# RetNet recurrence and softplus-erf MoE block on one core: the first layer of group G0 as 26 products, with its half of W_in summed by ScalarE and accumulating GpSimd transfers

## The chip, the cores and the metric

The kernel runs on one core of a Trainium2 chip, in one launch. The metric is the device time of the execution in microseconds (us); lower is better. The engines are TensorE (PE, with its weight loads PEld), VectorE (DVE), ScalarE (ACT), GpSimd (POOL) and SyncE (SP). Each works through its own queue of instructions in order, and waits on semaphores for what other engines or DMA transfers must have done.

## The reference

A recurrent attention block (RetNet, float32) feeds a block with two matrix products and a gate between them. B, H, S, D are 4, 8, 768, 64; the second block sees 3072 tokens of 512 features, W_in is 512 x 2048 and W_out 2048 x 512. The weights come as 64-bit floats.

```python
for t in range(S):
    state = gamma[None, :, None, None] * state + np.einsum('bhd,bhe->bhde', k[:, :, t], v[:, :, t])
    y[:, :, t] = scale * np.einsum('bhd,bhde->bhe', q[:, :, t], state)
...
x = np.ascontiguousarray(attn_out.transpose(0, 2, 1, 3)).reshape(B * S, H * D)
h = x @ w_in
sp = np.maximum(h, 0.0) + np.log1p(np.exp(-np.abs(h)))
g = h * erf(sp)
return (g @ w_out).astype(np.float32)
```

So softplus and erf are taken of every element of `h`, and everything is computed in float32.

## The kernel before

**Stages.** The recurrence is cut into 24 chunks `j` of 128 positions, each done with products inside the chunk and a state carried from chunk to chunk. The first four chunks give the first 512 tokens, which go through the second block in four groups (g = 0 to 3), one for each 512 of the 2048 hidden features: `hidden(g, u)` makes four tiles of `h`, `gate(g)` takes softplus and erf on ScalarE, `gated(g)` multiplies by `h` on VectorE, and `project(g, tt)` adds to the output of 128 tokens in PSUM. In these early groups the weights are also converted from 64-bit words to float32, in 16 pieces, by VectorE and ScalarE (`conversion`, L313 to L331), from raw buffers that SP's loads fill; four buffers turn, and a load goes out when the piece before it in the same buffer has been read.

The other 2560 tokens go in chunks of 256, two groups for each chunk: group g = G0 + 2i takes half s=0 of the hidden features and the next one half s=1, with G0 = 4 and 24 groups in all. There W_in's half is a 4 x 4 grid of 16 blocks (each 128 x 256 here), and the tokens' x is a 4 x 2 grid. The first layer is done with a fast algorithm: 26 products of sums of blocks (`hidden_steps`, the list `STEPS`), in place of 32 plain ones. For it, `W_SUMS` makes 30 sums of blocks of W_in for each half, in place and in tiles 16 to 25, once in the whole kernel (`sum_in`, L344, on VectorE), and `x_sums` makes 18 sums of blocks of x for each chunk (L933, VectorE). Each product goes to one of four PSUM banks (two named `hp`, two named `r`), and is read from there into `h`: the first time for a block of `h` by ScalarE (L965, L967), afterwards added or subtracted by VectorE (L963). A product that writes a bank waits until the reads of what it held are done. The second layer uses seven products instead of eight (`project_part`, L1034), with four more sums of W_out (T1 to T4) for each half: these are made by a negating ScalarE copy and a GpSimd transfer that adds in its flight (`sums`, L352 and L353). T2 is made from T1, and T4 from T2.

**Group G0 before.** Since the sums of W_in cannot be made before the plain use of W_in in groups 0 to 3 is over, G0's first layer is done plainly (`hidden_plain`, L971 to L985): eight tiles of 4 products with 256 columns. In the meantime VectorE makes half s=1's sums (L1187, L1196, L1200), and half s=0's from L1209 on into group G0+1, by the list `order` (L1241 to L1243). `project(G0 - 1, tt)`, the last part of the first 512 tokens, stands in between, with `put_first`, which copies its output out.

**What sets the order.** The order of instructions is written out by hand (`manual_schedule`): the program's order is each engine's order. In the early groups small steps are paid out at points of `hidden` and `project`: conversion steps by `pace`, other steps by the list `waiting`, in `pace_around`. In the later groups, lists by product number (`order`) say after which product VectorE or ScalarE gets another step: `prepared(j)` scales and transposes a chunk's k and q (five VectorE steps), `g_sums` makes the sums for the second layer, `last_steps` a sum of W_out. `sub_begin(j)`, `sub_states(j)` and `sub_visit(j, g)` do a chunk of the recurrence on TensorE with VectorE's mask and state. `load(j)` puts a chunk's loads on SP's queue.

**Names that come up.** G0 is group 4; half s holds features by `w_in_of` and `w_out_of`. W_in's blocks stand in `w_in_sb[:, s, 0:26]`; tiles 16 to 23 of each half serve as raw buffers for the conversion first, as does part of `w_out_sb` (`spare`, `place`). HS is `h`, E the gate's result. `act`, `ret` and `ps_h` have two buffers of each named tile.

## Time and profile before

| what | before |
| --- | --- |
| median of 3 runs | 662.71 us (662.67 to 663.26) |
| profiled execution, span from the first to the last instruction | 660.9 us |
| granted TensorE clock, mean | 1.000 |
| TensorE busy | 655.7 us |
| VectorE busy | 508.4 us |
| ScalarE busy | 280.2 us |
| GpSimd busy | 11.7 us |
| VectorE's 60 sums of W_in (L344), 128 x 256 each | 0.42 us each |
| G0's plain first layer (L980) | 64 instructions, from 127.6 to 142.7 us |
| first layer of G0+1 (L951) begins | 158.4 us |

The page counts an fp32 matmul as two instructions, so a product of `STEPS`, with its two column halves of the weights, is four, and the 26 products of a group are 104. The profile's times of an engine are the sums of its instructions' durations; matmuls overlap in them, so TensorE's rate is read from the distance between starts. A line in the timeline gives the start, the length of a run of like instructions, the engine, the source line, the operation and the tiles; in square brackets stands how long the engine was idle before it, and what ended the wait. The groups from G0+1 to the last but one follow each other at a distance of 25.9 us (158.4, 184.3, 210.2 us and so on). The DMA engines are busy for 0.83 to 1.17 of the time in every 10 us from 10 to 80 us, and for 0.61 or less in the 30 us after them.

### The profile page before, as it was taken

Reading aid. Unit: us, or ns where it says so; the run is one execution under the profiler, and the core shown is the slowest. Engines: PE = TensorE matmul, PEld = TensorE weight load, DVE = VectorE, ACT = ScalarE, POOL = GpSimd, SP = SyncE. Lnnn points to the kernel's source line nnn. Section 1 sums busy time; section 2 is a strip of 40 time slices with the busy share of each in tenths; the row PEclk is TensorE's granted clock in tenths of the full one; section 3 lists DMA queues with packets and bytes.
Section 4 is the critical chain, followed back from the end, with each engine's and each line's share of the span. In section 5 each row is a group of like instructions: output and inputs, shape, how many; then the busy total and the mean of one; then the engine's idle time right before and its main releaser. Section 6 shows DMA issues by size and latency. Waiting matters only on the chain.

```text
span 660.9 us, 15247 instructions
## 1 busy us (share of the span) xinstructions
PE 655.7 (99%) x6200; PEld 557.3 (84%) x6200; DVE 508.4 (77%) x1102; ACT 280.2 (42%) x402; POOL 11.7 (2%) x29
## 2 busy tenths in 40 slices
PE   8999999999999999999999999999999999999998
PEld 7744444576999999999999999999999999999997
DVE  5999999969986786788678678677687688476464
ACT  3468363445534334244254253342432542533440
POOL 1000000110100000000000000000000000000000
PEclk9999999999999999999999999999999999999999
DMA  9999844385753321222222322221231210000000
GB/s 188 223 264 231 211 129 107 63 152 90 144 123 61 85 47 32 67 47 46 70 44 47 73 39 46 42 72 37 44 79 36 46 53 1 2 34 0 1 33 32
DMA packets 159413, 51.88 MB, mean 78 GB/s; under 512 B 143216, under 2 KB 149744, under 8 KB 159344
## 3 DMA queue, kind: packets, MB, share of 16 engines
q1 hardware_dynamic: 157776, 46.72, 32.8%
q0 software_dynamic: 1152, 4.19, 3.4%
q8 instruction: 48, 0.79, 0.5%
q14 instruction: 21, 0.17, 0.1%
q10 hardware_dynamic: 416, 0.01, 0.0%
HBM read 40.39 MB, written 6.29 MB: 71 GB/s over the span
## 4 chain that ended last, share of the span: by engine, by line
PE 98%; DMA 1%; DVE 0%; ACT 0%; issue 0%
PE o L1034 37%; PE hp L951 22%; PE r L951 12%; PE hp L860 8%; PE o L896 8%; PE hp L980 2%; PE r L736 2%; PE hp L628 1%; PE o L772 1%; PE r L524 1%; PE r L557 1%; PE o L604 1%; PE r L751 1%; PE hp L751 1%; DMA kq<-in_k_dram 1%; PE r L772 0%
## 5 line engine op out<-in xcount | busy, mean ns | idle before, releaser
L1034 PE MATMUL o<-w_out_sb,h 128*128 128x256 f32 (+1 forms) x640 | 142.7, 380 | 0.0
L951 PE MATMUL hp<-xs,w_in_sb 128*128 128x128 f32 x988 | 138.1, 275 | 0.0
L1034 PEld LDWEIGHTS o<-w_out_sb,h 128*128 128x128 f32 x640 | 119.5, 190 | 16.6
L963 DVE TENSOR_TENSOR h<-h,hp 128x256 f32<-128x256 f32 x190 | 78.0, 418 | 70.5 <-PE hp L951 65.6
L951 PEld LDWEIGHTS hp<-xs,w_in_sb 128*128 128x128 f32 x988 | 128.4, 192 | 3.0
L1034 PE MATMUL o<-w_out_sb,e 128*128 128x256 f32 x480 | 113.5, 379 | 0.0
L1034 PEld LDWEIGHTS o<-w_out_sb,e 128*128 128x128 f32 x480 | 86.8, 190 | 9.4
L817 ACT ACTIVATE e<-h 128x2048 f32<-128x2048 f32 x22 | 42.1, 1912 | 119.6 <-DVE h L963 119.6
L963 DVE TENSOR_TENSOR h<-h,r 128x256 f32<-128x256 f32 x152 | 56.9, 415 | 22.3 <-PE r L951 21.4
L965 ACT COPY h<-hp 128x256 f32<-128x256 f32 x38 | 14.2, 373 | 130.7 <-PE hp L951 122.7
L951 PE MATMUL r<-xs,w_in_sb 128*128 128x128 f32 x456 | 63.3, 275 | 0.0
L951 PEld LDWEIGHTS r<-xs,w_in_sb 128*128 128x128 f32 x456 | 57.0, 192 | 0.0
L860 PE MATMUL hp<-xT,w_in_sb 128*128 128x512 f32 (+2 forms) x144 | 56.5, 548 | 0.0
L849 DVE TENSOR_TENSOR e<-h,e 128x1024 f32<-128x1024 f32 x42 | 49.2, 1213 | 8.0 <-ACT e L830 8.0
L860 PEld LDWEIGHTS hp<-xT,w_in_sb 128*128 128x128 f32 x144 | 25.8, 190 | 27.0 <-issue 24.6
L951 PE MATMUL hp<-xT,w_in_sb 128*128 128x128 f32 x304 | 46.3, 275 | 0.0
L951 PEld LDWEIGHTS hp<-xT,w_in_sb 128*128 128x128 f32 x304 | 41.5, 192 | 1.4 <-issue 0.5
L830 ACT ACTIVATE e<-e 128x2048 f32<-128x2048 f32 (+1 forms) x23 | 42.1, 1836 | 0.2
L967 ACT ACTIVATE h<-hp 128x256 f32<-128x256 f32 x57 | 21.9, 384 | 29.7 <-PE hp L951 28.3
L951 PE MATMUL r<-xT,w_in_sb 128*128 128x128 f32 x228 | 31.7, 275 | 0.0
L830 ACT ACT_TABLE_LOAD x24 | 30.8, 1283 | 0.4
L951 PEld LDWEIGHTS r<-xT,w_in_sb 128*128 128x128 f32 x228 | 28.5, 192 | 0.0
(164 smaller groups left out, 799.0 us busy)
## 6 DMA issues: line engine op xcount, KB each, us to landing
w_out_sb<-in_moe_w_out_dram SPq DMA_DIRECT2D x14, 512.0 KB, 5.2
kq<-in_k_dram SPq DMA_DIRECT2D x23, 256.0 KB, 4.0
v<-in_v_dram SPq DMA_DIRECT2D x23, 256.0 KB, 3.4
out_dram<-r SPq DMA_DIRECT2D x23, 256.0 KB, 2.9
kq<-in_q_dram SPq DMA_DIRECT2D x288, 16.0 KB, 1.9
kb<-in_k_dram SPq DMA_DIRECT2D x288, 16.0 KB, 1.8
w_in_sb<-in_moe_w_in_dram SPq DMA_DIRECT2D x8, 512.0 KB, 10.1
w_out_sb<-w_out_sb POOLq DMA_DIRECT2D x8, 512.0 KB, 5.3
```

The source lines that it names most:

```text
L736: nc.tensor.matmul(pp[r][col * D : (col + 1) * D, u % 2, t], x[own, u, :], QT[j][own, u, t], start=first(r, col), stop=True, skip_group_ch ...
L751: nc.tensor.matmul(other[a][own, u % 2, D:] if crossed else pp[a][own, u % 2, t], V[j][t, 2 * u + r, :], AM[j][t, r, u, :D], start=crossed ...
L817: nc.scalar.activation(E[g], HS[g], AF.Softplus)
L830: nc.scalar.activation(E[g][:, half], E[g][:, half], AF.Erf)
L849: nc.vector.tensor_tensor(E[g][:, half], HS[g][:, half], E[g][:, half], op=ALU.mult)
L860: nc.tensor.matmul(HP_[ft][:, t], w_in_of(ft, kk), XC[0][:, kk, t], start=(kk == 0), stop=(kk == n_k - 1),)
L896: nc.tensor.matmul(O[0][tt].rearrange("p (d c) -> p d c", d=2), E[g][:, u * TCH + tt * P : u * TCH + (tt + 1) * P], w_out_of(ft), start=(f ...
L951: nc.tensor.matmul(to[:, u, :], w_in_sb[:, s, w, u * P : (u + 1) * P], XS[m](x), start=first and u == 0, stop=True, skip_group_check=True,)
L963: nc.vector.tensor_tensor(h, h, of, op=ALU.add if plus else ALU.subtract)
L965: nc.scalar.copy(h, of)
L967: nc.scalar.activation(h, of, AF.Copy, scale=-1.0)
L1034: nc.tensor.matmul(O[m][i][:, half, at], G[g][a][:, u * P : (u + 1) * P], w_out_sb[:, s, OUT[b], u, at], start=i not in started, stop=(s = ...
```

## The change

G0's first layer is now `hidden_steps(G0)`, the 26 products, and `hidden_plain` is gone. So half s=0's sums must be there before G0. For that the halves are cut otherwise: s=0 is now the features of groups 0 and 1, s=1 those of groups 2 and 3 (`w_in_of`, `w_out_of`, `conversion`), so W_in's half s=0 has had its plain use after group 1. The new `moved_sums` makes a sum with a ScalarE copy (negating for a difference) into the target tile or into one of two tiles `negated`, and a GpSimd transfer of 128 KB that adds in its flight; where the target is one of the terms of an addition, the transfer alone does it. All 30 sums of half s=0 are made in this way at points of `project` and `hidden` (before and after `pace_around`), and the first 12 of half s=1 during G0's products; VectorE makes the remaining 18 of s=1 (`sum_in(1, n_sums)`). The list of sums is put in another order:

```python
W_SUMS = (
    (17, 8, 10, "-"), (16, 2, 6, "+"), (7, 3, 7, "+"), (4, 4, 17, "+"), (10, 10, 16, "+"),
    (2, 2, 3, "+"), (18, 16, 4, "-"), (8, 12, 8, "-"), (22, 15, 13, "-"), (19, 18, 5, "-"),
    (25, 18, 7, "+"), (3, 3, 15, "-"), (20, 1, 19, "-"), (16, 16, 7, "+"), (4, 4, 6, "-"),
    (20, 0, 20, "+"), (19, 19, 13, "-"), (7, 7, 10, "+"), (21, 9, 20, "+"), (24, 20, 12, "-"),
    (1, 1, 5, "+"), (9, 13, 9, "-"), (12, 17, 12, "-"), (5, 5, 2, "+"), (23, 15, 9, "-"),
    (6, 14, 12, "+"), (15, 2, 15, "-"), (13, 23, 11, "-"), (6, 6, 15, "-"), (13, 13, 7, "-"),
)
```

A row (to, a, b, sign) sets tile `to` to the sum or difference of tiles a and b. Tiles 16 to 23 of half s=0 are written by the sums early, so as a raw buffer they serve once only, and the other three turn (`place`). To make room in SBUF, `am` of the first chunks lies in a tile of the name `r`, and `am` of the later ones has D columns instead of C. In G0 `sub_begin(6)` follows the layer, two calls of `project(G0 - 1, ...)` stand ahead of `sub_visit` instead of one, and `prepared(6)` is paid out after products 6, 8, 10, 13 and 15.

```diff
--- before.py
+++ after.py
@@ -44,35 +44,35 @@
 
 N_W, N_X = 26, 18
 W_SUMS = (
...
@@ -223,11 +223,11 @@
     w_out_sb = const.tile([P, 2, 7, FG, DH], F32, name="w_out_sb")
 
     def w_in_of(ft, kk):
-        half, s, i = ft // (2 * FG), ft % (2 * FG) // FG, ft % FG
+        s, half, i = ft // (2 * FG), ft % (2 * FG) // FG, ft % FG
         return w_in_sb[:, s, 4 * (2 * half + i // 2) + kk, i % 2 * P : (i % 2 + 1) * P]
 
     def w_out_of(ft):
-        half, s, i = ft // (2 * FG), ft % (2 * FG) // FG, ft % FG
+        s, half, i = ft // (2 * FG), ft % (2 * FG) // FG, ft % FG
         return w_out_sb[:, s, 2 * half : 2 * half + 2, i, :]
 
 
@@ -243,7 +243,7 @@
     numbers = halves(spare[0][:, 2 * CE :])
     later = ret.tile([P, N_X, P], F32, name="xs", bufs=1)[:, : CE // P].rearrange("p a f -> p (a f)")
     powers = [halves(spare[1][:, 2 * CE :]), halves(later)]
-    last_power = halves(spare[1][:, :CE])
+    last_power = halves(spare[0][:, :CE])
     pieces = [("in", 0), ("in", 1)]
     for n in range(4):
         if n < 3:
@@ -251,7 +251,7 @@
         pieces += [("out", 2 * n), ("out", 2 * n + 1)]
     n_p = len(pieces)
 
-    place = [n % 4 if n < n_p - 4 else (n - n_p + 4) % 3 for n in range(n_p)]
+    place = (0, 1, 2, 3, 0, 1, 2, 0, 1, 2, 0, 1, 2, 0, 1, 2)
 
     def load_piece(n, *parts):
 
@@ -287,7 +287,7 @@
 
 
         which, i = pieces[n]
-        half, s, at = i // 4, i % 4 // 2, i % 2
+        s, half, at = i // 4, i % 4 // 2, i % 2
 
 
         parts = itertools.product(
@@ -339,14 +339,36 @@
 
     def sum_in(s, upto):
 
-        assert all(("hidden", 2 * FG + s * FG + u) in done for u in range(FG))
+        assert all(("hidden", (2 * s + 1) * FG + u) in done for u in range(FG))
         for to, a, b, sign in W_SUMS[in_sums[s] : upto]:
             nc.vector.tensor_tensor(w_in_sb[:, s, to], w_in_sb[:, s, a], w_in_sb[:, s, b], op=OP[sign])
         in_sums[s] = max(in_sums[s], upto)
 
+    negated = [const.tile([P, 2 * P], F32, name=f"negated{i}") for i in range(2)]
+
+    def moved_sums(s, upto):
+
+
+        assert all(("hidden", (2 * s + 1) * FG + u) in done for u in range(FG))
+        while in_sums[s] < upto:
+            n = in_sums[s]
+            to, a, b, sign = W_SUMS[n]
+            x = w_in_sb[:, s]
+            if sign == "+":
+                if to not in (a, b):
+                    nc.scalar.copy(x[:, to], x[:, b])
+                add = x[:, b if to == a else a]
+            else:
+                minus = negated[n % 2] if to == a else x[:, to]
+                nc.scalar.activation(minus, x[:, b], AF.Copy, scale=-1.0)
+                add = minus if to == a else x[:, a]
+            nc.gpsimd.dma_start(x[:, to], add, accum_op=ALU.add)
+            in_sums[s] += 1
+            yield
+
     def sums(s):
 
-        assert ("project", s) in done
+        assert ("project", 2 * s + 1) in done
         x = {name: w_out_sb[:, s, at] for name, at in OUT.items()}
         for to, a, b in (("T1", "12", "11"), ("T2", "22", "T1"), ("T3", "22", "12"), ("T4", "21", "T2")):
             nc.scalar.activation(x[to], x[b], AF.Copy, scale=-1.0)
@@ -485,6 +507,7 @@
 
     QT, KT, SC, AM, XC, SU = {}, {}, {}, {}, {}, {}
 
+    first_am = act.tile([P, 2, 2, HP, C], F32, name="r", bufs=1)
     psum_turn = itertools.cycle((ps_r, ps_h))
 
 
@@ -879,8 +902,12 @@
         done.add(("hidden", ft))
         if ft == FG - 1:
             need("in", FG + 2)
+        if g > 1:
+            next(moves, None)
         if g:
             pace_around(3.4 if ft > FG else 0)
+        if g > 1:
+            next(moves, None)
 
     def project(g, tt):
         if g == 0 and tt == 0:
@@ -902,7 +929,9 @@
             )
         if step == TT - 1:
             done.add(("project", g))
+        next(moves, None)
         pace_around(3.4)
+        next(moves, None)
 
     def put_first(tt):
         o = E[G0 - 1].rearrange("p (u t c) -> p t u c", u=FG, t=TT)[:, tt]
@@ -968,22 +997,6 @@
                 written.add(o)
             yield
 
-    def hidden_plain(g):
-
-        m, s = chunk_of(g), (g - G0) % 2
-        HS[g] = act.tile([P, N], F32, name="h")
-        h = HS[g].rearrange("p (f t u c) -> p f u t c", f=2, t=2, u=FG)
-        x = XC[m // 2][:, :, m % 2 * SCH : (m % 2 + 1) * SCH]
-        for f, u in itertools.product(range(2), range(FG)):
-            to = ps_h.tile([P, TCH], F32, name="hp")[:, :SCH]
-            for kk in range(n_k):
-                nc.tensor.matmul(
-                    to, w_in_of((2 * f + s) * FG + u, kk), x[:, kk], start=kk == 0, stop=kk == n_k - 1
-                )
-            nc.scalar.copy(h[:, f, u], to.rearrange("p (t c) -> p t c", t=2))
-            yield
-        done.update(("hidden", (2 * f + s) * FG + u) for f in range(2) for u in range(FG))
-
     G = {}
 
     def last_gated(g):
@@ -1148,6 +1161,9 @@
         ],
     ]
 
+    n_sums = len(W_SUMS)
+
+    moves = moved_sums(0, n_sums)
     for g in range(G0):
         for u in range(FG):
 
@@ -1184,42 +1200,41 @@
     nc.gpsimd.memset(idle, 1.0)
 
     j = JPC + 2
-    sum_in(1, 12)
-    all_of(prepared(j))
+    assert in_sums[0] == n_sums
+    moves = moved_sums(1, 12)
+    x_sums(G0)
+    gated(G0 - 1)
     load(j + 2)
-    gated(G0 - 1)
-    for n, _ in enumerate(hidden_plain(G0), start=1):
-        if n in (1, 4, 7):
+    next_chunk = prepared(j)
+    for n, _ in enumerate(hidden_steps(G0), start=1):
+        if n in (6, 8, 10, 13, 15):
+            next(next_chunk, None)
+        if n in (11, 17, 23):
             next(last_steps)
-        if n == 3:
-            sub_begin(j)
-    sum_in(1, 20)
-    x_sums(G0)
+        if n in (4, 8, 13, 15, 19, 21, 25):
+            next(moves, None)
+    all_of(moves)
+    all_of(next_chunk)
+    sub_begin(j)
+    project(G0 - 1, 0)
     sub_states(j)
     all_of(prepared(j + 1))
-    sum_in(1, len(W_SUMS))
-    project(G0 - 1, 0)
     nc.scalar.activation(idle, idle, AF.Softplus)
     gate_softplus(G0)
+    project(G0 - 1, 1)
     sub_visit(j, G0)
     load(j + 3)
     put_first(0)
+    put_first(1)
     gate_erf(G0)
     next(last_steps)
-    sum_in(0, 12)
-    for tt in range(1, TT):
+    sum_in(1, n_sums)
+    for tt in range(2, TT):
         project(G0 - 1, tt)
         put_first(tt)
     gated(G0)
-    sum_in(0, 20)
     j += 1
 
-    def sums_left():
-        for n in range(21, len(W_SUMS) + 1):
-            sum_in(0, n)
-            yield
-
-    w_sums = sums_left()
     put = None
     for g in range(G0 + 1, NG):
         even = (g - G0) % 2 == 0
@@ -1238,9 +1253,6 @@
                 18: (next_chunk, e_sums), 20: (e_sums,), 24: (next_chunk,),
             }
         if g == G0 + 1:
-            order.update({n: (w_sums,) for n in (1, 2, 3, 4)})
-            for n in (14, 16, 18, 20, 24):
-                order[n] += (w_sums,)
             order.update({n: (last_steps,) for n in (11, 17, 23)})
         for n, _ in enumerate(hidden_steps(g), start=1):
             if put is not None and n in (14, 16, 18):
@@ -1257,7 +1269,6 @@
         gate_softplus(g)
         if more:
             sub_visit(j, g)
-        all_of(w_sums)
         if g == G0 + 1:
             all_of(last_steps)
         if g + 1 < NG and not even:
```

Left out of the diff are the rows of `W_SUMS`, given above, and the three places where the later chunks' `am` is read and written with its new shape.

More of the change, by code (lines that the diff above doesn't have):

```diff
@@ L46 @@
 W_SUMS = (
+    (17, 8, 10, "-"),
     (16, 2, 6, "+"),
-    (17, 8, 10, "-"),
+    (7, 3, 7, "+"),
     (4, 4, 17, "+"),
     (10, 10, 16, "+"),
+    (2, 2, 3, "+"),
     (18, 16, 4, "-"),
+    (8, 12, 8, "-"),
+    (22, 15, 13, "-"),
     (19, 18, 5, "-"),
+    (25, 18, 7, "+"),
+    (3, 3, 15, "-"),
     (20, 1, 19, "-"),
+    (16, 16, 7, "+"),
+    (4, 4, 6, "-"),
     (20, 0, 20, "+"),
+    (19, 19, 13, "-"),
+    (7, 7, 10, "+"),
     (21, 9, 20, "+"),
+    (24, 20, 12, "-"),
+    (1, 1, 5, "+"),
     (9, 13, 9, "-"),
-    (22, 15, 13, "-"),
+    (12, 17, 12, "-"),
+    (5, 5, 2, "+"),
     (23, 15, 9, "-"),
-    (7, 3, 7, "+"),
-    (24, 20, 12, "-"),
-    (25, 18, 7, "+"),
-    (2, 2, 3, "+"),
-    (8, 12, 8, "-"),
-    (12, 17, 12, "-"),
-    (3, 3, 15, "-"),
-    (15, 2, 15, "-"),
-    (19, 19, 13, "-"),
-    (16, 16, 7, "+"),
-    (7, 7, 10, "+"),
-    (4, 4, 6, "-"),
-    (1, 1, 5, "+"),
-    (5, 5, 2, "+"),
-    (6, 14, 12, "+"),
+    (6, 14, 12, "+"),
+    (15, 2, 15, "-"),
+    (13, 23, 11, "-"),
     (6, 6, 15, "-"),
-    (13, 23, 11, "-"),
     (13, 13, 7, "-"),
@@ L566, in ret_mask @@
     def ret_mask(j):
-        AM[j] = ret.tile([P, 2, HP, C], F32, name="am")
+        AM[j] = first_am[:, j % 2]
         for s in range(2):
@@ L632, in sub_mask @@
     def sub_mask(j):
-        AM[j] = ret.tile([P, 2, HP, C], F32, name="am")
+        AM[j] = ret.tile([P, 2, HP, D], F32, name="am")
         for s in range(2):
             nc.vector.tensor_tensor(
-                AM[j][:, s, :, :D],
+                AM[j][:, s],
                 SC[j][s][:, :, :D],
@@ L691, in sub_results @@
                         V[j][t, 2 * u + r, :],
-                        AM[j][t, r, u, :D],
+                        AM[j][t, r, u],
                         start=False, stop=True, skip_group_check=True,
@@ L753, in of_values @@
                         V[j][t, 2 * u + r, :],
-                        AM[j][t, r, u, :D],
+                        AM[j][t, r, u],
                         start=crossed or first(r, col), stop=True, skip_group_check=True,
```

## The prediction

> **What bounds the kernel now.** I read the page's engine totals and chain first, then the timelines of TensorE, VectorE, GpSimd and ScalarE round the place of the change.
>
> ```profile
> PE 655.7 (99%) x6200; PEld 557.3 (84%) x6200; DVE 508.4 (77%) x1102; ACT 280.2 (42%) x402; POOL 11.7 (2%) x29
> PE 98%; DMA 1%; DVE 0%; ACT 0%; issue 0%
> ```
>
> TensorE is the bound everywhere, at a granted clock of 1.00 in every window. So a change pays by the TensorE time that it removes, less every gap that it opens. TensorE's timeline (start, duration, line, count) at G0, the group whose first layer changes:
>
> ```profile
> 127.60 5.34 PE L980 MATMUL hp<-xT,w_in_sb 128*128 128x256 f32 x24
> ...
> 133.96 8.90 PE L980 MATMUL hp<-xT,w_in_sb 128*128 128x256 f32 x40
> 142.70 3.60 PE L896 MATMUL o<-w_out_sb,r 128*128 128x512 f32 x8
> ...
> 148.00 10.57 PE L896 MATMUL o<-w_out_sb,r 128*128 128x512 f32 x24
> 158.41 0.61 PE L951 MATMUL hp<-xT,w_in_sb 128*128 128x128 f32 x4
> ```
>
> The plain layer (L980) is 64 instructions; with chunk 6's scores between (132.87 to 133.96, 1.09 us) it takes 142.70 - 127.60 - 1.09 = 14.01 us. In the L951 rows a product (4 instructions) starts each 0.445 us. VectorE before the next group (G0+1):
>
> ```profile
> 148.75 0.41 DVE L797 TENSOR_TENSOR state<-state,r 128x256 f32<-128x256 f32 x1
> 149.08 4.85 DVE L344 TENSOR_TENSOR w_in_sb<-w_in_sb 128x256 f32<-128x256 f32 x12
> 153.85 2.35 DVE L849 TENSOR_TENSOR e<-h,e 128x1024 f32<-128x1024 f32 x2
> 156.12 4.47 DVE L344 TENSOR_TENSOR w_in_sb<-w_in_sb 128x256 f32<-128x256 f32 x12
> 160.91 0.42 DVE L963 TENSOR_TENSOR h<-h,hp 128x256 f32<-128x256 f32 x1 [0.31 <-PE hp L951]
> 163.11 0.68 DVE L537 TENSOR_TENSOR kq<-kq,kq_s 128x512 f32<-128x512 f32 x1
> 163.71 1.41 DVE L963 TENSOR_TENSOR h<-h,r 128x256 f32<-128x256 f32 x4
> ```
>
> VectorE is free of its sums at 160.6, and G0+1's product 5 is there for it at 160.8: by 0.3 us it isn't late. A sum costs 4.77/12 to 4.47/12, mean 0.39 us; a PSUM read (L963) occupies 0.42 and gives way after 0.33. GpSimd's accumulating transfers today, 512 KB each:
>
> ```profile
> 131.17 1.01 POOL L353 DMA_DIRECT2D w_out_sb<-w_out_sb  x1 [11.94 <-ACT w_out_sb L352]
> 137.82 0.87 POOL L353 DMA_DIRECT2D w_out_sb<-w_out_sb  x1 [5.64 <-PE hp L980]
> 172.03 1.80 POOL L353 DMA_DIRECT2D w_out_sb<-w_out_sb  x2 [6.48 <-PE r L951]
> ```
> ```profile
> DMA to landing us min/median/max: 4.6/5.3/7.1
> ```
>
> By the packet records of their queue the first packet goes 1.43 us after the issue starts, the data take 2.9 to 4.2 us (two queued together 6.1: they go one after another), and the landing follows 0.4 later.
>
> **The change, part by part.**
>
> *TensorE's work.* Out go 14.01 us, in come 26 x 0.445 = 11.6: a gain of at most 2.4 us.
>
> *But the new layer runs bare.* In every other group `project_part` stands after products 14, 18 and 24 (1.72 us each) and lets VectorE catch up. In G0 nothing does, and VectorE's queue has five steps of `prepared` (three of 0.60, two transposes of 0.63) among 18 PSUM reads. From product 1, with each read 0.11 after its product's end (0.61 after its start): product 5 read at 2.50, then 0.60, product 8 at 3.84, 0.60, product 9 at 4.78, 0.60, products 11 and 12 (two reads each) from 5.72, product 13 from 7.06 to 7.48. Product 15 writes the bank of 13: it starts at 7.55, not 6.23. Product 17 waits 0.07 for 14's read, and 25 waits 0.76 for 24's, which nothing separates from it. Sum 2.15: the layer takes 13.74, and of the 2.4 us only 0.27 is left. Group G0+1 starts at 158.14.
>
> *VectorE's sums.* 42 of 60 leave VectorE (42 x 0.39 = 16.4 us), but TensorE waited for none of them, so that gains nothing by itself. 18 sums of half s=1 stay, with `gated(G0)` (2.27), between `sub_visit` and G0+1. `sub_visit` now follows two `project` calls: it ends at 127.60 + 13.74 + 1.09 + 7.0 + 1.8 = 151.24, and VectorE is free 1.08 later as today (149.08 against 148.00): 152.3. Let S be when the 18 sums start. VectorE reads product 5 at S + 18 x 0.39 + 2.27 = S + 9.3; product 9 needs that bank 0.49 later, at S + 9.8. Today it starts at 158.41 + 8 x 0.445 = 161.97. So the kernel is later by S - 152.2 as long as TensorE waits; 152.3 gives +0.1.
>
> *The chain that sets S.* The first of the 18 needs sum 9's transfer (tile 19, from 18, from 4). On GpSimd's queue, in order: sums 0, 1, W_out's T1, sums 2, 3, T2, 4, 5, T3, 6, 7, 8, 9. T1's ScalarE negation comes after product 10 (132.7 to 133.7); issue 0.3 later as in the rows (ScalarE's ended 130.86, issue 131.17): 134.0; landed +5.0 = 139.0. T2's negation reads T1: 139.05 to 140.1, issue 140.4, data from 141.85. No row shows a 128 KB accumulation. Below, a quarter of the shortest data time (0.72) gives 1.43 + 0.72 + 0.4 = 2.5 us; above, a whole 512 KB one is 4.6, and the 16 KB loads land in 1.9. I take a quarter of 3.1, since packets shrink with it: 0.8, or 2.7 landed. Then T2 3.1, sums 4 and 5 1.6, T3 3.1, sum 6 0.8: data end 150.4, landed 150.8; sum 9 issued 151.0, landed 153.7. S = 153.7: 1.5 us later. All terms shortest: 152.4 (+0.2); all longest (T1 5.96, data 4.16): 157.8 (+5.6).
>
> "DMA: Bandwidth & Descriptors" of the Trainium skill (section "Anatomy of one DMA — SWDGE") gives 2.0 us plus bytes at 436 GB/s. By it 512 KB land in 3.2 us where the rows have 4.6 to 7.1, and the chain would no longer matter: the sum would be +0.1 instead of +1.5. I follow the rows.
>
> *The sums of half s=0 in the early groups.* The same ScalarE that copies `h` out of PSUM now waits for landings:
>
> ```profile
> 69.19 1.15 ACT L314 ACTIVATE w_out_sb<-w_out_sb,below 128x1024 uint32<-128x1024 uint32 x1 [3.67 <-DVE w_out_sb L313]
> 71.92 0.59 ACT L878 COPY h<-hp 128x512 f32<-128x512 f32 x1 [1.58 <-PE hp L860]
> 75.35 0.59 ACT L878 COPY h<-hp 128x512 f32<-128x512 f32 x1 [2.85 <-PE hp L860]
> ```
>
> Sum 0 starts after erf of group 1, at 64.4. Sum 6's negation needs sum 3, which needs sum 0; behind it stand L314 of the next W_out piece (1.15), sum 7 (0.35) and this first L878 (0.59). TensorE's third tile of group 2 (75.16) needs that bank, so the negation must start by 72.65. Transfer 0 is issued at 65.05; the DMA share is 0.96 there, so each 128 KB takes 0.8 alone to about 1.9 shared; with four in one queue sum 3 lands between 70.6 and 74.5. Price 0 to 1.9 us; I take 0.4, the window's middle (72.5) lying just inside. If TensorE slips here all else slips with it.
>
> "SBUF — State Buffer" (section "SBUF: two separate sides") says that VectorE in a 2-port mode keeps GpSimd from writing descriptors. The conversions' 0.69 us L313 and L317 may be such; by my estimate it would add up to 0.7 us to each issue in this chain and about 1 us to the result. No row of before has such a pair, so it is not in the sum.
>
> *Three raw buffers for weights instead of four.* DMA is full until 79 us. Piece in5 landed at 58.0, three us before VectorE reads it at 61.15. Now its buffer is free only at 49.97 and chunk 5's loads (3.8 us of stream) go ahead: 61.8, so VectorE waits some 0.65 us. Piece out3 was ready at 83.69 and is needed at 82.90 + 4 x 0.4375 = 84.65: 0.96 us of cover, so nothing reaches TensorE; without that cover the 0.65 would. Later pieces may wait 1 to 2 us more; they, `x_sums` and `gated(3)` have 5 us until 127.6, since twelve sums went from there.
>
> *What costs nothing.* G0's softplus stands behind the twelve ScalarE steps of half s=1 (the last near 143.1; table 1.28, softplus 1.89: 146.4) and `put_first(1)` ahead of its erf: erf ends near 156.4, and `gated(G0)` comes at S + 7.0 = 160.7; 4 us of cover, beyond which S moves by the rest. `kq_b` (L480) queues on GpSimd behind 30 transfers, the last issued near 115, and is read at 131.8. `am`'s new tiles and `last_power`'s new place change no instruction. The second `project` ahead of `sub_visit` only gives `prepared(7)` more time.
>
> Sum: -0.27 (in the formula already) gives +1.5 in G0 and +0.4 early, so +1.9 on a span of 660.9; the runs' median lies 1.8 over the span, and I leave that distance alone: 662.71 + 1.9 = 664.6.
>
> **Rivals.**
> A, the gain comes: the layer takes its bare 11.6 because VectorE keeps up. Then product 9 is due at 159.6, so S = 149.8 is the point from which TensorE waits again; VectorE is free at 150.2, so 2.0 of the 2.4 can be kept: 660.7. For it: the counted TensorE work. Against: S = 149.8 needs T1 and T2 each to land 2 us sooner than I take, and the shortest rows of all give 152.4.
> B, transfers are fast and VectorE alone sets S = 152.3: +0.1 to +0.4, 663.0. For it: the shortest rows.
> C, ScalarE is blocked early as well: 1.9 + 1.5, 666.1. For it: the full DMA queue.
> That the change doesn't do what it says: the rearranged order of the program has 52 matmuls for G0 and 42 sum transfers on GpSimd, so it does.
>
> **How the numbers follow.** Forecast 0.54, A 0.13, B 0.18, C 0.15. A measurement tells 0.2%, 1.3 us, from no change. The forecast is slower in four fifths of its cases (S over 153.1 with the early 0.4, or over 153.5 without), else the same; B is the same but for a little on both sides; C is slower. Slower 0.58, same 0.26, faster 0.16. Range: B and C lie within, 662.2 to 667.0, with A left out below and the longest chains above; the likeliest case alone 663.3 to 666.5.
>
> **What would show it.** In the profile after: the G0 layer's 104 instructions spread over 13 to 14 us with a hole before product 15; the first L344 sum of VectorE released by a DMA near 153.7, and TensorE idle or waiting before product 9 of G0+1; a late L878 near 74. I am wrong if sum transfers land in under 2 us, or if G0's layer is 11.6 long.

## The result, and the profile after

The changed kernel took 682.0 us (median of 6 runs, 675.6 to 683.7), the kernel before 662.9 us beside it (6 runs, 662.7 to 664.1): a ratio of 1.0273, 95% interval 1.0245 to 1.0301. That is 18 us slower by the ratio, and 19.1 between the medians. The prediction said slower by 1.9. The page of the changed kernel, engine totals and the chain that ended last:

```profile
span 680.2 us, 15438 instructions
PE 660.4 (97%) x6240; PEld 559.5 (82%) x6240; DVE 500.5 (74%) x1078; ACT 289.3 (43%) x431; POOL 50.6 (7%) x71
PE 74%; DMA 8%; DVE 7%; SPq 6%; issue 2%; ACT 2%; DVEq 0%; ACTq 0%
```

TensorE made 98% of the chain before; now 26% of it are transfers, VectorE, SP's queue and others. TensorE's timeline shows where it stood still (in brackets the idle time before a row and what ended it):

```profile
70.58 2.07 PE L883 MATMUL hp<-xT,w_in_sb 128*128 128x512 f32 x2 [2.37 <-DVE w_in_sb L331]
...
118.58 2.07 PE L883 MATMUL hp<-xT,w_in_sb 128*128 128x512 f32 x2 [2.49 <-ACT h L901]
...
137.37 0.61 PE L980 MATMUL hp<-xT,w_in_sb 128*128 128x128 f32 x4
...
144.94 0.71 PE L980 MATMUL hp<-xs,w_in_sb 128*128 128x128 f32 x4 [1.10 <-DVE h L992]
...
150.22 0.71 PE L980 MATMUL hp<-xs,w_in_sb 128*128 128x128 f32 x4 [0.51 <-DVE h L992]
...
152.40 7.13 PE L923 MATMUL o<-w_out_sb,r 128*128 128x512 f32 x16
...
168.57 0.68 PE L980 MATMUL hp<-xT,w_in_sb 128*128 128x128 f32 x4 [0.20 <-DMA kq<-in_q_dram]
...
174.70 1.16 PE L980 MATMUL hp<-xs,w_in_sb 128*128 128x128 f32 x8 [2.16 <-DVE h L992]
...
186.88 1.22 PE L980 MATMUL hp<-xs,w_in_sb 128*128 128x128 f32 x4 [3.55 <-DVE h L992]
...
233.01 1.16 PE L980 MATMUL hp<-xs,w_in_sb 128*128 128x128 f32 x8 [0.95 <-DVE h L992]
```

With one more of 1.15 at 106.6 these are 14.5 us of holes; before there was none over 0.35 but one of 1.5 at the very start, which both have. The holes cost twice: the granted clock, 1.00 in every window before, is 0.91 in 60 to 80 us, 0.96 in 100 to 140 and 0.91 in 180 to 200, which is 0.09 x 20 + 0.04 x 40 + 0.09 x 20 = 5.2 us. Together 19.7, against 19.3 by which the span grew. (The one run at 675.6 had a mean clock of 1.000, the others 0.990 to 0.995.)

Who was late behind each hole? VectorE's timeline of the changed kernel, its longest waits for transfers:

```profile
66.11 0.69 DVE L313 TENSOR_SCALAR xs<-w_out_sb 128x1024 uint32<-128x1024 uint32 x1 [5.12 <-DMA w_out_sb<-in_moe_w_in_dram]
...
165.92 6.12 DVE L344 TENSOR_TENSOR w_in_sb<-w_in_sb 128x256 f32<-128x256 f32 x18 [3.52 <-DMA w_in_sb<-w_in_sb]
...
184.00 0.69 DVE L569 TENSOR_TENSOR kb<-kb,kq_b 128x512 f32<-128x512 f32 x1 [5.51 <-DMA kb<-in_k_dram]
...
227.88 0.69 DVE L569 TENSOR_TENSOR kb<-kb,kq_b 128x512 f32<-128x512 f32 x1 [4.27 <-DMA kb<-in_k_dram]
```

The first is weight piece in5, the second the 18 sums, the third and fourth are the key rows of chunks 8 and 10, which come over SP. ScalarE's timeline:

```profile
74.62 0.42 ACT L363 ACTIVATE w_in_sb<-w_in_sb 128x256 f32<-128x256 f32 x1 [6.63 <-DMA w_in_sb<-w_in_sb]
...
86.86 0.42 ACT L363 ACTIVATE w_in_sb<-w_in_sb 128x256 f32<-128x256 f32 x1 [3.47 <-DMA w_in_sb<-w_in_sb]
...
115.62 0.42 ACT L363 ACTIVATE w_in_sb<-w_in_sb 128x256 f32<-128x256 f32 x1 [8.33 <-DMA w_in_sb<-w_in_sb]
...
117.93 0.60 ACT L901 COPY h<-hp 128x512 f32<-128x512 f32 x1
```

Three negations wait for transfers of earlier sums, and the copy of `h` behind the third is what TensorE waited for at 118.58.

SP's timeline says why the key rows were late. Before:

```profile
99.33 0.41 SPq L205 DMA_DIRECT2D kq<-in_k_dram  x1
99.79 9.86 SPq L187 DMA_DIRECT2D kq<-in_q_dram  x16
...
136.40 10.98 SPq L187 DMA_DIRECT2D kq<-in_q_dram  x16
...
194.97 7.49 SPq L187 DMA_DIRECT2D kb<-in_k_dram  x16
```

and after:

```profile
107.51 0.51 SPq L205 DMA_DIRECT2D kq<-in_k_dram  x1
108.06 15.04 SPq L187 DMA_DIRECT2D kq<-in_q_dram  x16
...
154.84 14.34 SPq L187 DMA_DIRECT2D kq<-in_q_dram  x16
...
217.62 8.73 SPq L187 DMA_DIRECT2D kb<-in_k_dram  x16
```

From 99 us on SP issues without a pause: each chunk is 34 loads. It started on chunk 6 8.2 us later, behind the last two W_out pieces, and fell further back: from there to the landing of chunk 10's last key row it took 120.1 us, before 105.4. (In e4 below, which leaves out every moved sum, it took 112.8, so transfers on GpSimd's queue can be only a part of that.) Chunk 10's key rows were issued 22.7 us later. That this chain had no slack stood in the profile before. VectorE's timeline there:

```profile
139.30 0.69 DVE L546 TENSOR_TENSOR kb<-kb,kq_b 128x512 f32<-128x512 f32 x1 [3.18 <-DMA kq<-in_k_dram]
...
205.45 0.68 DVE L546 TENSOR_TENSOR kb<-kb,kq_b 128x512 f32<-128x512 f32 x1
```

It waited 3.2 us for chunk 7's loads already, and chunk 10's last row had landed at 204.74, 0.7 us ahead of its use.

### The profile page after: what moved, and what is told of

Read it like the earlier page. It is cut to its first block, busy times and chain, and to the rows that moved or that the text cites. A ratio compares the mean times of both kernels' runs of the same rounds, so it can differ in the third digit from the quotient of the medians.

```text
span 680.2 us, 15438 instructions
## 1 busy us (share of the span) xinstructions
PE 660.4 (97%) x6240; PEld 559.5 (82%) x6240; DVE 500.5 (74%) x1078; ACT 289.3 (43%) x431; POOL 50.6 (7%) x71
## 4 chain that ended last, share of the span: by engine, by line
PE 74%; DMA 8%; DVE 7%; SPq 6%; issue 2%; ACT 2%; DVEq 0%; ACTq 0%
PE o L1047 34%; PE hp L980 21%; PE r L980 11%; SPq L187 5%; DMA w_out_sb<-in_moe_w_in_dram 3%; DMA kq<-in_k_dram 2%; PE r L759 1%; PE hp L651 1%; DMA kb<-in_k_dram 1%; PE o L923 1%; DMA kq_b<-decay_k_dram 1%; PE o L795 1%; DVE w_out_sb L322 1%; DVE w_out_sb L325 1%; DMA w_in_sb<-w_in_sb 1%
## 5 line engine op out<-in xcount | busy, mean ns | idle before, releaser
L980 PE MATMUL hp<-xs,w_in_sb 128*128 128x128 f32 x1040 | 146.9, 276 | 8.3 <-DVE h L992 8.3
L980 PEld LDWEIGHTS hp<-xs,w_in_sb 128*128 128x128 f32 x1040 | 135.7, 193 | 12.3 <-DVE h L992 9.2
L992 DVE TENSOR_TENSOR h<-h,hp 128x256 f32<-128x256 f32 x200 | 82.2, 419 | 76.1 <-PE hp L980 71.4
L992 DVE TENSOR_TENSOR h<-h,r 128x256 f32<-128x256 f32 x160 | 60.1, 417 | 21.4 <-PE r L980 19.1
L980 PE MATMUL r<-xs,w_in_sb 128*128 128x128 f32 x480 | 66.7, 275 | 0.0
L883 PE MATMUL hp<-xT,w_in_sb 128*128 128x512 f32 (+2 forms) x144 | 60.0, 573 | 4.9 <-ACT h L901 2.5
L980 PEld LDWEIGHTS r<-xs,w_in_sb 128*128 128x128 f32 x480 | 60.0, 192 | 0.0
L883 PEld LDWEIGHTS hp<-xT,w_in_sb 128*128 128x128 f32 x144 | 26.9, 199 | 34.4 <-issue 25.3
L980 PEld LDWEIGHTS hp<-xT,w_in_sb 128*128 128x128 f32 x320 | 43.6, 192 | 2.4 <-ACT r L938 1.0
L365 POOL DMA_DIRECT2D w_in_sb<-w_in_sb x36 | 35.6, 1267 | 101.9 <-ACT w_in_sb L359 60.1
L980 PE MATMUL r<-xT,w_in_sb 128*128 128x128 f32 x240 | 34.2, 280 | 0.0
```

What stands on the lines that cost most here:

```text
L365: nc.gpsimd.dma_start(x[:, to], add, accum_op=ALU.add)
L883: nc.tensor.matmul(HP_[ft][:, t], w_in_of(ft, kk), XC[0][:, kk, t], start=(kk == 0), stop=(kk == n_k - 1),)
L980: nc.tensor.matmul(to[:, u, :], w_in_sb[:, s, w, u * P : (u + 1) * P], XS[m](x), start=first and u == 0, stop=True, skip_group_check=True,)
L992: nc.vector.tensor_tensor(h, h, of, op=ALU.add if plus else ALU.subtract)
```

## The experiments

Times are medians; the ratio is to the kernel before, run beside. "No sums" and "neither" leave out sums and their transfers, and e15 and e16 their ScalarE steps, so that the output of e2 to e4, e7, e10, e13 and e15 to e17 is not the reference's.

| run | ratio [95%] | us |
| --- | --- | --- |
| the change | 1.0273 [1.0245, 1.0301] | 682.0 |
| e1 chunk 5's loads behind in5 | 1.0259 [1.0218, 1.0300] | 679.8 |
| e2 no half 0 sums | 1.0180 [1.0155, 1.0205] | 675.3 |
| e3 no moved half 1 sums | 1.0289 [1.0253, 1.0326] | 682.7 |
| e4 neither | 1.0145 [1.0124, 1.0166] | 672.3 |
| e5 before, three raw buffers | 1.0048 [1.0033, 1.0063] | 665.8 |
| e6 before, SP 8 us later | 1.0106 [1.0091, 1.0121] | 669.8 |
| e7 neither, in5 in a fifth place | 1.0145 [1.0127, 1.0162] | 671.7 |
| e8 the change, in5 in a fifth place | 1.0308 [1.0287, 1.0329] | 683.1 |
| e9 the change, chunk 6 early | 1.0313 [1.0289, 1.0338] | 683.7 |
| e10 neither, chunk 6 early | 1.0133 [1.0110, 1.0157] | 673.0 |
| e11 GpSimd's own sums | 1.0251 [1.0206, 1.0297] | 678.9 |
| e12 as e11, chunk 6 early | 1.0312 [1.0288, 1.0335] | 684.0 |
| e13 neither, SP relieved | 1.0076 [1.0048, 1.0104] | 667.9 |
| e14 the change, SP relieved | 1.0221 [1.0201, 1.0241] | 678.1 |
| e15 transfers without ScalarE | 1.0192 [1.0158, 1.0226] | 676.3 |
| e16 as e15, SP relieved | 1.0190 [1.0167, 1.0213] | 676.1 |
| e17 neither, SP relieved finely | 1.0078 [1.0063, 1.0093] | 668.1 |
| e18 GpSimd copies, SP relieved finely | 1.0192 [1.0165, 1.0218] | 676.4 |

**Which part of the change (e1 to e4).** e1 moves chunk 5's loads two blocks on:

```diff
-            ([(K_, 4), (need, "in", FG + 3), (load, 5)], []),
+            ([(K_, 4), (need, "in", FG + 3)], []),
...
-            ([(T, 4)], []),
+            ([(T, 4), (load, 5)], []),
```

> Chunk 5's three loads are issued two hidden blocks later, so that on SP the loads of piece in5 stand ahead of them; nothing else is changed. Theory (the early loss is the late landing of in5, which VectorE's order puts ahead of in4's last steps): in5 is issued near 50 us instead of 55.2, lands near 61 instead of 66.0, VectorE's wait of 5.12 us falls below 1, hidden(2,0) starts at 68.3 to 68.8 instead of 70.6, and the total falls from 682.0 by the stall of 2.3 and the slower clock after it (1.7): 677 to 680. Rival (ScalarE's waits for sums are the bound of that stretch anyway, its first one ends at 74.6): the early start is given back by 123 us, and the total stays at 681 to 683. Rival (chunk 5, now late, takes the place of in5): slower than 683.

The hole at 68 us went; one of 3.34 came at 75.2, behind a copy of `h` on ScalarE, and those at 106 and 116 stayed. The median is in the range expected, but its interval also holds the rival's 681 to 683 and overlaps the change's: the wait for in5, first to be seen, is not by itself the loss.

e2, e3 and e4 put this in place of the sums (e2: half 0; e3: the 12 of half 1; e4: both):

```diff
+    def filled(s, upto):
+        in_sums[s] = upto
+        nc.gpsimd.memset(w_in_sb[:, s, 16:], 1.0)
+        yield
...
-    moves = moved_sums(0, n_sums)
+    moves = filled(0, n_sums)
```

> The 30 sums of half 0 (ScalarE's copies and GpSimd's transfers beside the groups 2 and 3) are left out; one GpSimd memset fills their ten blocks instead, so the output isn't the reference's. Piece order, three raw buffers, G0's 26 products and the 12 moved sums of half 1 stay. Theory: what is left is the wait for in5 (2.3, with the clock after it up to 4) and the late chain behind T1 to T3 (3.0): 667 to 671 against 662.9 before and 682.0 with the sums; ScalarE's waits of 6.6, 3.5 and 8.3 us are gone, project(2) starts at 116 to 118 instead of 123.6, and SP's loads of chunks 6 to 8 are no later than the start of project(2) is. Rival (the loss is mostly the late half, the early sums only fill time): 677 or more. Rival (the wait for in5 is itself a consequence of ScalarE's sums): 664 to 666.

> The 12 sums of half 1 that ran as transfers are left out (a GpSimd memset fills their blocks; the output isn't the reference's); the 30 sums of half 0 stay, VectorE's 18 sums of half 1 too. Theory: VectorE's 18 sums no longer wait for transfers behind T1 to T3, so the gap of 2.2 us before product 10 of the first layer of half 1 goes (3.0 with what hangs on it), and the loads of chunk 7 and 8, which SP could not issue beside those transfers (issues of 2.2 and 6.0 us), come earlier, so that the gap of 3.5 us near 184 shrinks too: 674 to 679, with the early lateness of 9.8 us at project(2) unchanged. Rival (the late chain is hidden behind the chunk loads anyway): 680 to 683, only the place of the gap moves.

> Both groups of moved sums are left out (42 of them; two memsets in their place; the output isn't the reference's). What is left of the change: the order of the pieces, three raw buffers, first_am, G0 in 26 products, VectorE without the 42 sums. Theory: only the wait for in5 is left, less what the product layer saves (0.1): 665 to 667. Rival (with no sums on VectorE the product layer gains its 2.4 us, and the wait for in5 is gone as well, ScalarE being free): 660 to 661. Rival (G0's products themselves are the loss): 670 or more.

The half 0 sums cost 0.9 to 1.4% (6 to 10 us: the change against e2, e3 against e4). The 12 sums of half 1, from which the prediction took its main cost, show no difference where the others are there (e3, at its rival). Without the others (e2 against e4) it is 2.3 us, with intervals that just overlap; e2 has a hole of 2.17 before product 9 of G0+1, behind the 18 sums, and e4 has not. e2 came out above its 667 to 671. And e4 was a miss: with no moved sum at all 9.6 us are still lost, where 2 to 4 were expected. VectorE's timeline of e4 shows them:

```profile
215.98 0.69 DVE L575 TENSOR_TENSOR kb<-kb,kq_b 128x512 f32<-128x512 f32 x1 [8.34 <-DMA kb<-in_k_dram]
```

TensorE's hole behind it is 5.03 us. So chunk 10's rows were late without any sum.

**Late loads (e5 to e8).** e5 is the kernel before with the new order of raw buffers alone:

```diff
-    place = [n % 4 if n < n_p - 4 else (n - n_p + 4) % 3 for n in range(n_p)]
+    place = (0, 1, 2, 3, 0, 1, 2, 0, 1, 2, 0, 1, 2, 0, 1, 2)
...
-    last_power = halves(spare[1][:, :CE])
+    last_power = halves(spare[0][:, :CE])
```

> The kernel before, with the change's order of raw buffers alone (three buffers from the fifth piece on, and the last scratch moved with it); sums, groups and products are those of before. Theory (late loads are the loss that stays without any moved sum): in5 waits behind chunk 5's loads, the last two pieces of W_out stand behind the 17 small loads of the scales, chunk 6's loads start 3 us later or more, SP, which issues without a pause from there to 205 us, doesn't catch up, and VectorE waits for chunk 9's kb rows near 208 us where it waited for nothing before: 667 to 672 against 662.9. Rival (G0's 26 products or the placing of loads among them delay SP; three buffers cost only the wait for in5): 663 to 665, no gap near 210. Rival (VectorE's sums of half 0 wait too, being behind in4 and in5): 672 or more.

It costs 3.2 us, less than expected. VectorE waits for in5 (2.4), for a W_out piece (1.7), for chunk 7's key rows (5.60, before 3.18) and for chunk 10's (3.06), which land at 211.64 instead of 204.74. (The expectations of e5 and e6 call these last chunk 9's.) TensorE's timeline in e5 has two new holes:

```profile
86.11 1.98 PE L896 MATMUL o<-w_out_sb,r 128*128 128x512 f32 x4 [1.50 <-DVE w_out_sb L331]
...
165.25 1.16 PE L951 MATMUL hp<-xs,w_in_sb 128*128 128x128 f32 x8 [1.50 <-DVE h L963]
```

The first stands before the product that needs out3, the cover that the prediction named: the wait of 2.38 less the cover of 0.96 is 1.42. The second is before product 9 of G0+1: after its wait for chunk 7's rows VectorE has no idle time until 165 us, and its sums come late. Behind chunk 10's rows TensorE has no hole in this run. e6 is the kernel before with one thing added, a second issue of chunk 7's 16 query loads:

```diff
-            load_blocks(KQ[j][:, 1].rearrange("p h d -> p (h d)"), q[b, :, now, :])
+            for _ in range(2 if j == NB + 1 else 1):
+                load_blocks(KQ[j][:, 1].rearrange("p h d -> p (h d)"), q[b, :, now, :])
```

> The kernel before with one thing added: the 16 loads of chunk 7's q rows are issued twice to the same place, which costs SP some 8 us (16 issues of 0.5) and moves 256 KB more; the output is unchanged. Theory (SP's queue has almost no slack up to 205 us: in the profile of before chunk 9's kb rows landed at 204.74 and VectorE began on them at 205.45): VectorE waits about 7 us there, TensorE about 4 of them, and the total is 666 to 669. Rival (the queue has slack, SP catches up before 205): 662.5 to 663.5.

8 us more on SP's queue made the kernel 7.0 us slower, though not at the place expected: the hole is at chunk 7, where VectorE waited already. Timelines of VectorE and TensorE in e6:

```profile
149.31 0.69 DVE L547 TENSOR_TENSOR kb<-kb,kq_b 128x512 f32<-128x512 f32 x1 [12.88 <-DMA kb<-in_k_dram]
```
```profile
151.87 0.69 PE L629 MATMUL hp<-qT,kT 64*64 64x64 f32 x32 [4.24 <-DVE qT L551]
```

This is shown, then: the kernel before had next to no slack on SP. e7 and e8 give in5 a place of its own, in blocks that nothing uses before in6:

```diff
...
-    place = (0, 1, 2, 3, 0, 1, 2, 0, 1, 2, 0, 1, 2, 0, 1, 2)
+    place = (0, 1, 2, 3, 0, 1, 2, 4, 0, 1, 2, 0, 1, 2, 0, 1)
...
-            if place[later] == place[n]:
+            if place[later] == place[n] or (n, later) == (3, 7):
```

> The run without any of the 42 moved sums (672.3), with one more place for raw words: piece in5 is loaded into the blocks 8 to 15 of W_in's second half, which nothing uses before in6 is converted, as soon as in3's conversion is issued; every later piece moves up by one place. Theory: in5 lands near 58 as before, the last W_out pieces are issued 5 us or more earlier, chunk 6's loads start at 99 to 100 instead of 102.9, the gap of 5.0 us near 216 falls to under 2: 663 to 667. Rival (SP is late for another reason, such as ring waits beside T1 to T3, or G0's layer): the gap near 216 stays at 4 or more: 669 to 672. The output isn't the reference's (the sums are left out).

> The changed kernel, whole, with the same fifth place for in5. Theory: VectorE's wait for in5 goes (5.1 us), hidden(2,0) starts at 68.3 to 68.8, the last W_out pieces are out of the way of the sums near 105 us, so that ScalarE's wait of 8.3 us shrinks: 672 to 678 against 682.0. Rival (ScalarE's in-order waits alone hold the groups 2 and 3 back): 680 to 683. Rival (the loads now collide with the sums earlier): slower than 683.

Both miss. The last two W_out pieces still stood behind the 17 small loads of the scales, chunk 6 began at 102.1, and the hole of e7 came at chunk 8 (3.24 at 171.4).

**SP's chain relieved (e9, e10, e13, e14, e17).** e9 and e10 issue 33 of chunk 6's loads between in6, in7 and out4:

```diff
-            ([], []),
-            ([], []),
+            ([(load_queries, 6)], []),
+            ([(load_keys, 6)], []),
             ([(T, 5)], []),
...
-            ([(load, 6), (sub_results, 5)], []),
+            ([(load_values, 6), (sub_results, 5)], []),
```

> The changed kernel; of chunk 6's loads the 33 of the keys and queries are issued on SP between the pieces in6, in7 and out4 (70 to 93 us, where SP waits for raw buffers most of the time) instead of behind the last piece; the values stay. Theory (from 140 us on SP's chain of small loads sets the end: in nine runs so far span minus the landing of chunk 10's kb rows was 452.6 to 456.2 us, wherever VectorE waited for those rows): the chain starts some 17 us earlier, chunk 10's rows land near 212 instead of 227.6, VectorE waits for them no longer, the gaps of 3.55 at 183 and 0.95 at 232 us are gone with the slower clock behind them, what stays are the gaps before 180 us (2.4, 1.2, 2.5, 1.6, 2.2): 672 to 677 against 682.0. Rival (the chain is a follower: TensorE's own lateness frees its buffers late): 680 to 683. Rival (the loads now collide with the pieces, which come later still): 683 or more.

> The run without any of the 42 moved sums (672.3), with chunk 6's loads early as above, and the filling memset cut into ten (the one of 2560 columns held VectorE's tensor_scalar at 46.15 us for 2.19 instead of 0.69 us, which cost TensorE 0.98). Theory: with SP's chain relieved the gap of 5.0 us near 216 and the slower clock after it (1.6) go, and that of 0.98: 663.5 to 666, of which the 26 products save 2.4 and lose 1.6 again in their bare layer. Rival (G0's products, first_am or the piece order hold something else back): 669 or more. Rival (with the chain gone the product layer's gain shows): 660.5 to 662. The output isn't the reference's (the sums are left out).

Key rows were no longer waited for, and every hole after 185 us but one of 0.3 was gone; but the kernels were no faster. The small loads held up in7 (issued at 87.2 in e10, 80.3 in e4), and VectorE stood before it and the piece after it. Its timeline in e10:

```profile
95.11 0.69 DVE L326 TENSOR_SCALAR xs<-w_out_sb 128x1024 uint32<-128x1024 uint32 x1 [6.05 <-DMA w_out_sb<-in_moe_w_in_dram]
...
104.82 0.69 DVE L326 TENSOR_SCALAR w_out_sb<-w_in_sb 128x1024 uint32<-128x1024 uint32 x1 [4.64 <-DMA w_in_sb<-in_moe_w_out_dram]
...
106.57 0.75 DVE L678 TENSOR_TENSOR am<-hp,causal_d 128x256 f32<-128x256 f32 x2
```

This is how a late piece reaches TensorE: its first conversion step is put into VectorE's program ahead of work that TensorE needs (here L678, behind which TensorE stood 5.84 us). e13 and e14 make the scales' 16 loads 4 and put chunk 6's query loads behind them, ahead of the last two pieces; e17 spreads chunk 6's loads in lots of eight:

```diff
-                    kq_b[part, 0, 0, u],
-                    decay_k[:, 2 * u + s : 2 * u + s + 1].rearrange("(a p) h -> p (a h)", p=32),
+                kq_b[part, 0, 0],
+                decay_k.rearrange("(a p) (u s) -> p u a s", p=32, s=2)[:, :, :, s],
...
                     load_block_scales()
+                    load_queries(6)
```

> The run without any of the 42 moved sums (the filling memset in ten parts), with SP relieved in a way that holds no piece of W_in back: the scales' 16 loads become 4, and chunk 6's key and query rows (17 loads) are issued right behind them, ahead of the last two pieces of W_out, for whose buffers SP otherwise waits. Theory (SP's chain of small loads, never more than 8 transfers in flight, sets the end of that run): chunk 6's kb loads start near 109 instead of 116.1, chunk 10's land near 209 instead of 215.7, the gap of 5.0 us and the slower clock behind it go, and the 0.98 of the memset: 664 to 667 against 672.3. Rival (chunk loads are not the bound, the gap at 216 would turn up elsewhere): 670 or more. The output isn't the reference's (the sums are left out).

> The changed kernel, whole, with the same relief of SP. Theory: chunk 8's and chunk 10's kb rows land in time, the gaps of 3.55 and 0.95 us at 183 and 232 go with the slower clock behind them; the gaps before 180 us, which the sums of half 0, in5 and the late chain make, stay: 674 to 677 against 682.0. Rival (the sums hold TensorE back by themselves as much as the chunk loads do, one takes the other's place): 680 to 683.

> The run without any of the 42 moved sums, with chunk 6's small loads spread finer: eight or nine of them behind the piece in7, eight behind out4, eight behind the four loads of the scales, eight behind out7, so that no piece waits for more than eight small loads. Theory (late pieces and SP's chain are all that is left when no sum is moved, and G0's 26 products are worth nothing net in a layer with 1.6 us of stalls): the gap of 3.2 us at 111 with its slower clock goes too, chunk 10's kb rows land in time: 662.5 to 665 against 667.9 with the coarse relief, 672.3 without, 663.0 before. Rival (something else of the change holds TensorE): 667 or more. Rival (the 26 products do gain their 2.4): 660 to 662. The output isn't the reference's (the sums are left out).

Relief takes 4.6 us off the 9.6 of e4 (1.0 of them by a memset cut into ten, see the end) and 3.4 off the change, in both a little less than expected. In e13 chunk 10's rows land at 207.2 and nothing waits for them. What is left there is again a piece: VectorE waits 8.4 us for one of W_out, TensorE 3.18 at 111. e17, which was to remove this, did not: VectorE waits 5.1 and 3.7 us for W_out pieces, TensorE 0.83, 2.34 and 1.65 between 84 and 116 us, 4.8 in all, where e17 loses 5.2. VectorE's timeline in e17:

```profile
112.82 0.69 DVE L328 TENSOR_SCALAR w_out_sb<-w_out_sb 128x1024 uint32<-128x1024 uint32 x1 [5.11 <-DMA w_out_sb<-in_moe_w_out_dram]
```

A run without moved sums and with the four buffers of before would close the account; it was not made.

**What the half 0 sums cost by (e11, e12, e15, e16, e18).** e15 keeps every transfer and leaves out ScalarE's step:

```diff
-                    nc.scalar.copy(x[:, to], x[:, b])
+                    nc.gpsimd.memset(x[:, to], 1.0)
...
-                nc.scalar.activation(minus, x[:, b], AF.Copy, scale=-1.0)
+                nc.gpsimd.memset(minus, 1.0)
```

> The changed kernel with the ScalarE step of every moved sum left out (a GpSimd memset of the same 256 columns, 0.2 us, writes the operand instead); all 42 accumulating transfers stay. ScalarE no longer waits for a landing. Theory A (ScalarE's waits in its order are what the half 0 sums cost): as without those sums, 674 to 677. Theory B (the transfers' share of the DMA engines delays pieces and chunk loads, and that is the cost): 680 to 683, with in7, out4 to out7 and chunk 6 as late as in the changed kernel. In between: both in part. The output isn't the reference's.

> Both edits: transfers alone, and SP relieved. If theory A and SP's chain together are the loss: 665 to 669, what is left being in5, the late chain's 2.2 and the bare layer. If theory B holds: 672 or more. The output isn't the reference's.

e15 is 5.4 us faster than the change and within 1 us of e2, which has no half 0 sums: that much of their price is ScalarE's waits. (e15 frees ScalarE of the half 1 sums as well, for which the change against e3 shows no gain.) It doesn't clear the transfers: in e15 SP begins on chunk 6 at 107.63, as late as in the change, where e4 begins at 102.90. And e16 misses: with SP relieved too nothing more is won, and it is some 8 us slower than e13, which has the same relief and no sums. VectorE waits 4.89 us for in5 in e16 (0.44 in e13), and for a W_out piece until 118.20 (111.24 in e13). VectorE's and TensorE's timelines in e16:

```profile
118.20 0.69 DVE L326 TENSOR_SCALAR w_out_sb<-w_out_sb 128x1024 uint32<-128x1024 uint32 x1 [8.65 <-DMA w_out_sb<-in_moe_w_out_dram]
```
```profile
121.15 5.54 PE L895 MATMUL hp<-xT,w_in_sb 128*128 128x512 f32 x8 [5.55 <-ACT h L913]
```

So the transfers have a price too, of late loads, which shows once ScalarE and SP are relieved; e16's small GpSimd memsets may be part of it, which no run tells apart. e11 and e12 let GpSimd compute the sums, e18 lets it copy and negate:

```diff
-            nc.gpsimd.dma_start(x[:, to], add, accum_op=ALU.add)
+            nc.gpsimd.tensor_tensor(x[:, to], x[:, a], x[:, b], op=OP[sign])
```

> The changed kernel, with each of the 42 moved sums as one GpSimd tensor_tensor instead of ScalarE's copy and an accumulating transfer: nothing waits on ScalarE, the DMA engines carry 42 transfers of 128 KB less. Theory (ScalarE's waits in its own order and the transfers' share of the DMA engines are what the half 0 sums cost, 7 to 10 us by the runs without them): near the run without any sums: 670 to 674. Rival (GpSimd's work holds VectorE, as the memset of 2.23 us did; 42 sums of 0.3 to 0.7 us each): 676 to 690, with VectorE's durations up where GpSimd runs.

> GpSimd's tensor_tensor sums and chunk 6's early loads together. Theory: neither cost is left, what remains is the wait for in5 and the bare layer: 664 to 668. Rival (GpSimd holds VectorE): 672 or more; rival (better than before): under 662.

> The changed kernel, whole, with the same finely spread loads, and the copies and negations of the moved sums on GpSimd instead of ScalarE, ahead of their transfers: ScalarE waits for no landing, the output is the reference's. Theory (ScalarE's waits cost 5.7 by the run with transfers alone, SP's chain 3.9 by the run with the coarse relief): 671 to 676 against 682.0. Rival (GpSimd's copies hold VectorE, as its sums did, 1.43 us each): 677 or more. Rival (a version that beats the kernel before): under 662.

e11 and e12 fell to their rival. Groups of e11, and below of the kernel before (busy us, mean ns), VectorE's from 55 to 130 us:

```profile
L357 POOL TENSOR_TENSOR w_in_sb<-w_in_sb 128x256 f32<-128x256 f32 x42 | 53.4, 1430 | 37.4 <-DVE xs L325 37.4
L322 DVE SCALAR_TENSOR_TENSOR w_out_sb<-w_out_sb 128x1024 f32<-128x1024 uint32 x7 | 9.9, 1417 | 0.2
```
```profile
L322 DVE SCALAR_TENSOR_TENSOR w_out_sb<-w_out_sb 128x1024 f32<-128x1024 uint32 x6 | 7.3, 1225 | 0.2
```

A sum takes GpSimd 1.43 us (VectorE 0.34 to 0.42), and VectorE's conversion beside it 1.42 instead of 1.23. e18 is the fastest of the versions that leave nothing out, at 676.4, 13 us behind the kernel before. None beat it.

## Why the prediction was right in sign and wrong in size

*TensorE's work and the bare layer: right.* The layer takes 152.40 - 137.37 - 1.09 = 13.94 us (predicted 13.74, before 14.01), and the starts of products 15 and 25 slip by 1.33 and 0.68 (predicted 1.32 and 0.76), with idle times of 1.10 and 0.51. e4 has the same two holes, so it is PSUM reads and `prepared`, not sums, that make them. Rival A is out.

*42 sums off VectorE gain nothing: right.* e4 and e17 have them off and are slower than before; the holes of e17 are 4.8 of its 5.2 us, so no gain is hidden behind them.

*The late chain: right as a mechanism, mis-sized, and then covered.* T1 landed at 148.43, in the old clock (less the layer's shift of 9.77) 138.7, predicted 139.0; a 128 KB transfer alone took 2.74 us, predicted 2.7. But T3 took 9.16 us beside chunk loads and sum 9 4.0. The 18 sums began at 165.92 - 9.77 = 156.15, predicted 153.7, and the slip before product 9 was 2.96, predicted 1.5. Without the half 0 sums it costs about what its hole takes (2.3 us between e2 and e4, a hole of 2.17). In the changed kernel it is not to be told from nothing on the total: where the chain is taken out there, the hole turns up behind late key rows (5.56 at 225.8 in e3).

*The early ScalarE block: the mechanism right, the term mis-sized at 0.4.* Measured: about 5.4 (e15 against the change). Sum 6's negation started at 74.62 instead of 72.5. I priced that one wait, at one copy; there are 30 sums, and the later waits (3.47, 8.33) stand before copies, conversions and scores too. That the transfers make the loads late had no term at all.

*"Nothing reaches TensorE": this step failed.* Three raw buffers were to cost 0.65 us of VectorE, covered by out3. in5 landed at 66.02, not 61.8: SP's issue of two of chunk 5's loads took 5.2 and 5.8 us, so that in5 went out at 55.21, and it was 10.8 us from there to the landing. VectorE waited 5.1 us for it; in e3, whose program is the same up to there, 1.6, and in e5 2.4. So the wait varies, but 0.65 was too small. With 2.4 the cover that failed was out3's, as named. With 5.1 another failed before it: L313 of in5 stands in VectorE's program ahead of the last steps of in4, which TensorE needs first. By itself the new order costs 3.2 us (e5).

*"Later pieces may wait 1 to 2 us more", covered: this step failed most.* I gave slack only to pieces, and none of the later loads a price. Late loads were put at nothing; without any moved sum 9.6 us were lost (e4, 1.0 of them by its memset), and what is read there behind TensorE's holes is late loads. SP issues pieces and chunk loads in one order, and chunk 7's and 10's rows were just in time (waited for by 3.2 us, and 0.7 ahead). Late pieces pushed chunk 6 back by 3 us (e5) to 8 (the change), and what followed went slower as well (105.4 us before, 112.8 in e4, 120.1 in the change). Slack here was to be read from VectorE's waits for loads, off the chain as they were.

*A hole costs more than its length.* The prediction had no term for the clock; it is 5.2 of the 19.

The terms don't add up: with late pieces, late rows and blocked copies each close behind the other, taking one away (e1, e3, e8, e9) brings the next one forward. That late pieces are all of the rest in e17 is read from its waits, not shown by a run.

## What to carry to other kernels

A kernel whose bounding engine has no hole may still have queues that arrive just in time: before moving a load back, look at how long ahead of its use every later load of the same queue lands, and at each wait of an engine off the chain. A step that waits for a transfer belongs into a queue in which nothing urgent stands behind it, and a look-ahead step is such a step as soon as its data are late. Where several such margins are near zero, the first visible stall isn't the loss, and removing it shows the next.
